# A delta-rule attention with a mixture of experts behind it: the first two triangular solves go from GpSimd to VectorE

## The chip, the cores and the metric
The kernel runs on one core of a Trainium2 chip. Five engines work side by side, each on its own instruction list in order: PE (TensorE, matmul), ACT (ScalarE), DVE (VectorE), POOL (GpSimd) and SP (SyncE, which here issues nearly all DMAs). They meet through semaphores. The metric is the device time in microseconds; before the change the median of three runs is 1027.19 us.

## The reference
Attention with a recurrent 40x40 state for each of 4 batches x 8 heads over 768 steps, then a top-2 mixture of 8 experts:

```python
for t in range(S):
    y[:, :, t] = einsum('bhd,bhde->bhe', r_t, state)
    Sa = einsum('bhde,bhe->bhd', state, a_t)
    state = state * w_t[:, :, None, :] - einsum('bhd,bhe->bhde', Sa, b_t) + einsum('bhd,bhe->bhde', v_t, k_t)
# x = y as [3072, 320]; logits = x @ w_gate, noise_scale = log1p(exp(x @ w_noise)),
# noisy = logits + noise_scale * noise; top 2 of 8 by noisy, softmax of the two;
# out = sum over the two experts of weight * (relu(x @ w1[e]) @ w2[e])
```

## The kernel before
The recurrence is done in chunks of 64 steps. The 12 chunks of 2 batch pairs (p = 0, 1) make 24 iterations (`for n in range(N)` in `run`), which run in order, since each hands the state on to the iteration two later of its pair. Four iterations (two chunks of both pairs) form a group g = 0 to 5, which is prepared together:

- `prepA(p,g)` loads w, b and a (`raww`, `rawba`), forms running products of w (`Gx`, a scan on VectorE), their inverses and the scaled operands, writes them to DRAM as pairs of 16-bit numbers (`pk` to `d_ab`) and reads them back stacked (`st_ab`). `rawba` and `Gx` have one buffer each, so that the next pair's load waits for the last use by this one. In groups 0 and 1 the two products of `rawba` run on VectorE, later on POOL.
- `scoresL` forms the 32x32 blocks on PE and writes them to DRAM (`scr<-lt`, `scr<-lo`) for both pairs.
- `tsolve(g)` reads them as one tile `X` (128 partitions, one 32x32 triangular matrix each, one buffer), masks it (L535), sets the diagonal (L536) and inverts it in 30 pairs of dependent instructions (L541 the outer product into `Tt`, L542 its sum into `X`). A pair j works on j x (31-j) elements, 30 to 240. The result goes to `th` (ACT L544, then VectorE L545), to DRAM, and from there into `dT`, four DMAs for each iteration (`fetchB`, L567).
- `prepC(p,g)` does the same as prepA for k (`rawk`).

An iteration (`chain`, then `outp`, and `pre` and `blocks` for the next) needs its `dT`: in `chain` the first application (PE pQ), a second block column, the split `w2` (ACT L598, VectorE L599, the second of the two `w` of an iteration), the second application, and the new state (L652). Iteration 0 needs group 0's solve, iteration 4 group 1's, iteration 8 group 2's.

The order on each engine is set once, when the program is built, by a scheduler that works from priorities and a model of times: what stands first in an engine's list runs first, and an instruction that waits holds up all behind it. `high_priority(offset)` puts instructions ahead in that choice; `add_manual_dep` without a semaphore only fixes an order. After the 24 iterations the experts run (some 450 us, nearly all PE); the change doesn't touch them.

Of the kernel before, what the change touches and what calls it, by code (L numbers as in the profile page):

```python
# [13 lines left out]
ALU = mybir.AluOpType  # L14
# [330 lines left out]
NP,NG,CG,C=2,6,2,64  # L345
# [3 lines left out]
SC=2.0**9; IS=2.0**-9  # L349
# [19 lines left out]
def host_tm(x):  # L369

    B,H,S,D=x.shape
    return np.ascontiguousarray(x[:,HS].reshape(NP,2,H,NG*CG,C,D).transpose(0,3,1,4,2,5)).reshape(NP,NG*CG,128,H*D)

class Att:
    PSC=1; PACC=3; PT=2; PPB=1
    def __init__(s,nc,tc,ctx,aps):
# [45 lines left out]
        for z in s.Sst+[s.Ut]: nc.vector.memset(z,0.0)  # L422
        s.dm=t([128,320],F16,name="dm"); nc.vector.memset(s.dm,0.0)

    def pack(s,src,scl,h,nc_,out):

        nc=s.nc
        pk=s.tmp.tile([120,nc_*2,X//nc_],F16,name="pk",bufs=PKB)
        v=pk.rearrange("p (c l) x->p c l x",l=2); sv=src.rearrange("p (c x)->p c x",c=nc_)
        nc.scalar.activation(v[:,:,h],sv,AF.Copy,scale=scl)  # L430
        nc.vector.scalar_tensor_tensor(v[:,:,1-h],sv,scl,v[:,:,h],op0=ALU.mult,op1=ALU.subtract)
        out(pk)
    def burst(s,f):

# [20 lines left out]
            return st[:,o:o+128] if b is None else st[:,o+64*b:o+64*b+64]  # L455
        return f
    def prepA(s,p,g):
        nc=s.nc; FM=s.aps[0]
        sh=[120,NS,64]; W0=NS*65
        w=s.inp.tile([120,W0],F32,name="raww",bufs=2); nc.sync.dma_start(w,FM[p,g][:,:W0])  # L460
        ba=s.inp.tile([120,2*X],F32,name="rawba",bufs=BAB)
        for i in range(2): nc.sync.dma_start(ba[:,X*i:X*i+X],FM[p,g][:,W0+X*i:W0+X*i+X])
        b_,a_=ba[:,:X],ba[:,X:]
        Gx=s.tmp.tile([120,NS,65],F32,name="Gx")
        fl=lambda z: z.rearrange("p a b->p (a b)")
        nc.vector.tensor_tensor_scan(fl(Gx),w,fl(s.d1),0.0,op0=ALU.mult,op1=ALU.add)
# [22 lines left out]
        (nc.vector if g in MD else nc.gpsimd).tensor_tensor(b_,b_,fl(NH),op=ALU.mult)
        s.pack(b_,-SC,1,1,lambda pk: nc.sync.dma_start(dv[:,:,1],pk))  # L490
        (nc.vector if g in MD else nc.gpsimd).tensor_tensor(a_,a_,fl(NG_),op=ALU.mult)
        s.pack(a_,-SC,0,1,lambda pk: nc.sync.dma_start(dv[:,:,0],pk))
# [12 lines left out]
    def prepC(s,G,gate=None):
        nc=s.nc; FM=s.aps[2]; p,g=G['p'],G['g']
# [171 lines left out]
    def run(s,m,xo=None):  # L678
        nc=s.nc
# [25 lines left out]
        with after(xd),(after(tl) if TG else ExitStack()):  # L705
            prepA(1,0); prepA(1,1); prepT(1)
# [3 lines left out]
        for n in range(N):  # L710
            g,c,p,cc=idx(n); ga,qa=divmod(n+LA,4); gc,qc=divmod(n+LC,4)
# [27 lines left out]
PT_=0; PA_=0  # L739
# [13 lines left out]
MD=(0,1); MG=(); MK=(0,); TG=0  # L753
# [128 lines left out]
```

## Time and profile before

| what | us |
|---|---|
| median of 3 timed runs (1023.14 to 1027.94) | 1027.19 |
| profiled execution | 1021.33 |
| its span, first to last instruction | 1019.5 |
| first `w2` of iteration 0 on VectorE | 152.24 |
| the last iteration's output `xt` on VectorE | 571.23 |

Busy over the span: PE 767.5 us (75%), DVE 492.1 (48%), ACT 396.1 (39%), POOL 521.4 (51%). These shares average over three stages that differ: up to 153 us almost nothing but preparation, from 153 to 571 us the iterations with the later groups' preparation between them, then the experts.

### The profile page before, as it was taken

The page shows a single profiled execution, that of the slowest core. Times are in us where ns is not written, and L with a number is a line of the kernel's source. Part 1 is how long each engine was busy: PE and PEld are TensorE (multiplying, and loading weights), DVE is VectorE, ACT ScalarE, POOL GpSimd, SP SyncE. Part 2 cuts the span into 40 slices and gives each one's busy share as a digit, 9 for nine tenths or more (in the row PEclk, how much of TensorE's full clock was granted, in tenths as well). Part 3 has the DMA queues.
Part 4 walks back from the last instruction along what each step waited for, and adds up shares of the span by engine and source line. Part 5 has one row for each costly group of instructions (what it writes and reads, how often), then busy time and mean ns, then how long its engine had stood idle before and what let it go on. Part 6 is the DMA issues. An engine that isn't in the chain of part 4 may idle for free.

```text
span 1019.5 us, 25178 instructions
## 1 busy us (share of the span) xinstructions
PE 767.5 (75%) x10506; PEld 681.2 (67%) x10506; DVE 492.1 (48%) x961; ACT 396.1 (39%) x816; POOL 521.4 (51%) x678
## 2 busy tenths in 40 slices
PE   0110117687877687899799379999999999999995
PEld 0110116576666576787688259899999989999995
DVE  9329525355567556447355542643434334443430
ACT  2213213354444344554454322543434334343421
POOL 6259979237967728818874335133333333333313
PEclk9999999797778787999899779999999999999998
DMA  3799963478479557655355843426262525262303
GB/s 96 188 203 226 242 172 90 116 197 225 127 193 241 146 121 204 175 152 146 96 120 148 272 119 68 131 49 150 49 150 49 150 49 149 50 149 51 36 7 40
DMA packets 135264, 136.21 MB, mean 134 GB/s; under 512 B 67392, under 2 KB 114948, under 8 KB 135060
## 3 DMA queue, kind: packets, MB, share of 16 engines
q1 hardware_dynamic: 123492, 117.35, 43.6%
q0 software_dynamic: 11648, 17.15, 9.6%
q8 instruction: 85, 1.39, 0.6%
q14 instruction: 39, 0.32, 0.1%
HBM read 96.48 MB, written 41.37 MB: 135 GB/s over the span
## 4 chain that ended last, share of the span: by engine, by line
PE 43%; POOL 21%; DMA 14%; issue 8%; DVE 6%; SPq 3%; ACT 3%; POOLq 0%; DVEq 0%; ACTq 0%
PE po L295 16%; PE ph L273 12%; POOL Tt L541 7%; POOL X L542 7%; PE pY L441 2%; PE psc L441 2%; PE pW L441 2%; DMA X<-scr 2%; DMA xr<-xd,le 2%; DMA out_dram<-y,le 2%; DMA d_ab<-pk 2%; DMA rawk<-in_fm_dram 2%; PE pt L254 2%; POOL rawk L515 2%; POOL xr L241 1%
## 5 line engine op out<-in xcount | busy, mean ns | idle before, releaser
L297 POOL DMA_INDIRECT out_dram<-y,le x56 | 92.4, 1651 | 201.2 <-ACT y L296 171.9
L276 DVE SCALAR_TENSOR_TENSOR hl<-ph,hh 128x256 fp32r<-128x256 f32 (+1 forms) x128 | 71.0, 556 | 154.0 <-ACT hh L274 153.6
L274 ACT ACTIVATE hh<-ph 128x320 fp32r<-128x320 f32 (+1 forms) x128 | 66.1, 518 | 156.1 <-PE ph L273 155.9
L541 POOL TENSOR_TENSOR Tt<-X 128x30 f32<-128x30 f32 (+9 forms) x180 | 108.8, 604 | 11.8
L542 POOL TENSOR_TENSOR X<-X,Tt 128x30 f32<-128x30 f32 (+9 forms) x180 | 106.3, 590 | 12.6
L241 POOL DMA_INDIRECT xr<-xd,le x56 | 54.0, 965 | 74.4 <-DMA le<-ls 27.9
L441 PEld LDWEIGHTS <-st_ab 120*64 120x64 f16 (+1 forms) x928 | 26.5, 117 | 75.8 <-issue 42.2
L295 PE MATMUL po<-w2h,hh 128*128 128x320 f32 x384 | 74.6, 314 | 0.0
L441 PE MATMUL pQ<-w,dT 128*128 128x40 f16 x1152 | 41.2, 184 | 42.3 <-DMA dT<-scr 33.5
L273 PE MATMUL ph<-xh,w1h 128*128 128x512 f32 (+1 forms) x256 | 71.3, 362 | 0.5 <-ACT xh L257 0.5
L441 PEld LDWEIGHTS <-dT 128*128 128x128 f16 x1152 | 38.2, 100 | 49.6 <-DMA dT<-scr 34.4
L273 PE MATMUL ph<-xh,w1l 128*128 128x512 f32 (+1 forms) x256 | 69.0, 351 | 0.0
L273 PE MATMUL ph<-xl,w1h 128*128 128x512 f32 (+1 forms) x256 | 68.6, 349 | 0.0
L295 PE MATMUL po<-w2l,hh 128*128 128x320 f32 x384 | 68.3, 312 | 0.0
L295 PE MATMUL po<-w2h,hl 128*128 128x320 f32 x384 | 68.1, 309 | 0.0
L441 PE MATMUL psc<-st_ab 120*64 120x64 f16 x384 | 12.6, 215 | 68.1 <-DMA st_ab<-d_ab 29.6
L295 PEld LDWEIGHTS po<-w2h,hh 128*128 128x128 f32 x384 | 61.3, 188 | 3.1
L441 PE MATMUL psc<-RV,uT 128*64 128x128 f32 x384 | 56.5, 294 | 4.1 <-DVE P L665 3.7
L295 PEld LDWEIGHTS po<-w2h,hl 128*128 128x128 f32 x384 | 59.2, 188 | 0.1
L295 PEld LDWEIGHTS po<-w2l,hh 128*128 128x128 f32 x384 | 58.9, 188 | 0.4
L162 POOL DMA_INDIRECT ls<-ent,po x48 | 47.2, 984 | 19.3 <-issue 13.6
L441 PE MATMUL psc<-RV 128*64 128x128 f32 x384 | 56.6, 294 | 0.0
(285 smaller groups left out, 1893.9 us busy)
## 6 DMA issues: line engine op xcount, KB each, us to landing
w2r<-in_w_dram SPq DMA_DIRECT2D x8, 1280.0 KB
RV<-in_rv_dram SPq DMA_DIRECT2D x48, 192.0 KB
rawba<-in_fm_dram SPq DMA_DIRECT2D x24, 360.0 KB
d_ab<-pk SPq DMA_DIRECT2D x24, 360.0 KB
st_ab<-d_ab SPq DMA_DIRECT2D x36, 240.0 KB
w1r<-in_w_dram SPq DMA_DIRECT2D x8, 1024.0 KB
raww<-in_fm_dram SPq DMA_DIRECT2D x12, 365.6 KB
st_ab<-d_ab SPq DMA_DIRECT2D x24, 180.0 KB
```

The source lines that it names most:

```text
L162: st=nc.gpsimd.indirect_dma_start(out=s.ls[s.half],out_offset=OFFS(ap=po[:,j,k:k+1],axis=0),in_=s.ent[:,j,k],in_offset=None)
L241: for k in range(c,c+a): nc.gpsimd.indirect_dma_start(out=x[:p,k],out_offset=None,in_=s.xd[w],in_offset=OFFS(ap=li[:p,k,0:1],axis=0))
L254: for t,p in tiles(t0,n): nc.tensor.transpose(pt[:,t-t0:t-t0+p],x[:p,t//128,f0:f0+128],s.idm[:p,:p])
L273: for i,(a,b) in enumerate(mm): nc.tensor.matmul(ph[:,:n],a,b,start=i==0,stop=i==7)
L274: nc.scalar.activation(hh[:,f,:n],ph[:,:n],AF.Relu)
L276: if c.stop>c.start: nc.vector.scalar_tensor_tensor(o,ph[:,c],0.0,hh[:,f,c].bitcast(F32),op0=ALU.max,op1=ALU.subtract)
L295: nc.tensor.matmul(po[:p],h[:,f,r],w[:,f],start=k==0,stop=k==23); k+=1
L297: st=nc.gpsimd.indirect_dma_start(out=s.out_d,out_offset=OFFS(ap=idx[:p,ii],axis=0),in_=y[:p],in_offset=None,compute_op=ALU.add)
L441: def mm(s,*a,**k): return lambda: s.nc.tensor.matmul(*a,**k)
L515: k1=k_[:,:,:,64*b:64*b+64]; (nc.vector if g in MK else nc.gpsimd).tensor_tensor(k1,k1,G['NH'].rearrange("p (a c b) t->p b c a t",a=3,c=CG ...
L541: eng.tensor_tensor(t,Xt[:,j:j+1,j+1:].to_broadcast([128,j,m]),Xt[:,0:j,j:j+1].to_broadcast([128,j,m]),op=ALU.mult)
L542: s.tl=eng.tensor_tensor(Xt[:,0:j,j+1:],Xt[:,0:j,j+1:],t,op=ALU.add)
```

## The change
All solves ran on POOL (`TPOOL`); now those of groups 0 and 1 run on VectorE. Group 0's gets a high priority offset, and a wrapper puts every VectorE instruction of group 1's `prepA` behind the last step of group 0's solve in VectorE's list. The rest of `prepA`'s lines change `nc.vector` to the wrapped `V`. In the changed kernel lines from L374 on stand 11 lower (L541 is L552), and the wrapped instructions are recorded at L380.

```diff
+class Behind:
+    def __init__(s,tc,eng,first): s.tc,s.eng,s.first=tc,eng,first
+    def __getattr__(s,name):
+        f=getattr(s.eng,name)
+        def g(*a,**k):
+            i=f(*a,**k)
+            s.tc.add_manual_dep(i.ins,s.first.ins.name,mybir.DependencyInfo(mybir.DependencyClass.NoSync,mybir.DependencyReason.DATA),reason="behind")
+            return i
+        return g
...
     def prepA(s,p,g):
-        nc=s.nc; FM=s.aps[0]
+        nc=s.nc; FM=s.aps[0]; V=Behind(s.tc,nc.vector,s.tl) if g==1 else nc.vector
...
-        nc.vector.tensor_tensor_scan(fl(Gx),w,fl(s.d1),0.0,op0=ALU.mult,op1=ALU.add)
+        V.tensor_tensor_scan(fl(Gx),w,fl(s.d1),0.0,op0=ALU.mult,op1=ALU.add)
...
         def prepT(g):
-          with s.tc.high_priority(offset=PT_):
+          with s.tc.high_priority(offset=PT_ if g else BURST):
             scr2[g]=s.tsolve(scr[g],nc.gpsimd if g in TPOOL else nc.vector)
...
-TPOOL=(0,1,2,3,4,5)
+TPOOL=(2,3,4,5)
```

VectorE's list at the place of group 0's solve, before: the last two scalings of k for group 0, then `ak` and `w` of iteration 0, `wg` (a constant of the experts' gate, loaded by DMA), `ak` of iteration 1, and group 1's `prepA` from `Gx` on.

```order
L431 SCALAR_TENSOR_TENSOR pk<-rawk,pk 120x2x384
L515 TENSOR_TENSOR rawk<-rawk,NH 120x6x64 x2
L431 SCALAR_TENSOR_TENSOR pk<-rawk,pk 120x2x384
L580 TENSOR_TENSOR ak<-psc,mk_124 128x512
L599 SCALAR_TENSOR_TENSOR w_870<-pW,w_870 128x320
L60 SCALAR_TENSOR_TENSOR wg<-wgn,wg 128x48
L580 TENSOR_TENSOR ak<-psc,mk_124 128x512
L466 SCALAR_TENSOR_TENSOR Gx<-raww,d_108 120x780
L472 TENSOR_TENSOR NH<-Gx,raww 120x768
L474 SCALAR_TENSOR_TENSOR raww<-NH,raww 120x768
L475 TENSOR_TENSOR NH<-raww,Gx 120x768
L482 TENSOR_TENSOR nge_556<-Gx,raww 120x12
```

The same place now (`X` and `Tt` are the solve's; `w`, `wg` and `ak` the same as above):

```order
L552 TENSOR_TENSOR Tt<-X 128x150
L553 TENSOR_TENSOR X<-X,Tt 128x6x25
L552 TENSOR_TENSOR Tt<-X 128x168
L553 TENSOR_TENSOR X<-X,Tt 128x7x24
L552 TENSOR_TENSOR Tt<-X 128x184
L610 SCALAR_TENSOR_TENSOR w_870<-pW,w_870 128x320
L60 SCALAR_TENSOR_TENSOR wg<-wgn,wg 128x48
L553 TENSOR_TENSOR X<-X,Tt 128x8x23
L591 TENSOR_TENSOR ak<-psc,mk_124 128x512
L552 TENSOR_TENSOR Tt<-X 128x198
L553 TENSOR_TENSOR X<-X,Tt 128x9x22
L552 TENSOR_TENSOR Tt<-X 128x210
```

The 62 instructions of the solve stand between the scalings of k and group 1's `Gx`; the two `ak`, `w` and `wg` stand inside it, and `Gx` comes after its last step.

VectorE's list at group 1's solve, before: iterations 1 and 2 (`w_1648` is iteration 2's first split, `Sst_171` the state after iteration 1, `P` the masked scores of iteration 1's output) and group 3's `prepA`, and in it `th` of group 1, which waits for POOL's solve.

```order
L599 SCALAR_TENSOR_TENSOR w_1648<-pW,w_1648 128x320
L474 SCALAR_TENSOR_TENSOR raww<-NH,raww 120x768
L652 SCALAR_TENSOR_TENSOR Sst_171<-pS,gam_146 128x8x40
L475 TENSOR_TENSOR NH<-raww,Gx 120x768
L482 TENSOR_TENSOR nge_2520<-Gx,raww 120x12
L445 COPY uT<-pu 128x512
L606 TENSOR_TENSOR sfs<-Sst_171,sfs 128x320
L481 COPY nge_4046<-nge_2520 120x6
L545 SCALAR_TENSOR_TENSOR th<-X,th 128x1024
L665 TENSOR_TENSOR P<-psc,mk 128x512
L431 SCALAR_TENSOR_TENSOR pk<-rawba,pk 120x768
L665 TENSOR_TENSOR P<-psc,mk 128x512
```

Now, at the start of that solve:

```order
L109 SCALAR_TENSOR_TENSOR xT<-px,xT 128x384
L442 SCALAR_TENSOR_TENSOR pk<-rawba,pk 120x768 x2
L663 SCALAR_TENSOR_TENSOR Sst_171<-pS,gam_146 128x8x40
L546 TENSOR_TENSOR X<-X,tri 128x1024
L617 TENSOR_TENSOR sfs<-Sst_171,sfs 128x320
L610 SCALAR_TENSOR_TENSOR w_1648<-pW,w_1648 128x320
L547 MEMSET X 128x32
L552 TENSOR_TENSOR Tt<-X 128x30
L456 COPY uT<-pu 128x512
L553 TENSOR_TENSOR X<-X,Tt 128x30
L552 TENSOR_TENSOR Tt<-X 128x58
L514 COPY gam_145<-pg 128x9x2
```

The 62 instructions of the solve now stand in VectorE's list from behind `Sst_171` of iteration 1 on; between its mask and its last step stand 28 others, 16 of iterations 1 to 3 and 12 of preparation. In front of its mask, all of group 1's and most of group 2's `prepA` stand between the two solves, mixed with iterations 0 and 1: 14 instructions of these from iteration 0's `w2` on.

SyncE's list at the load of group 1's matrix, before (`scr_433<-th` is group 0's inverse, `dT` its use in iterations 0 to 2):

```order
L492 DMA d_ab<-pk 120x2x768
L462 DMA rawba<-in_fm_dram 120x768 x2
L518 DMA d_k<-pk 120x4x384
L509 DMA rawk<-in_fm_dram 120x768
L534 DMA X<-scr 128x1024
L547 DMA scr_433<-th 128x2048
L567 DMA dT_147<-scr_433 32x8x64 x4
L567 DMA dT_148<-scr_433 32x8x64 x4
L567 DMA dT_147<-scr_433 32x8x64 x4
```

Now (`xd<-xt` is iteration 0's output, `dT_148` in front the load for iteration 3):

```order
L540 DMA scr<-lt 32x16x32
L540 DMA scr<-lo 32x16x32
L529 DMA d_k<-pk 120x4x384
L105 DMA xd_840<-xt 128x320
L578 DMA dT_148<-scr_433 32x8x64 x3
L545 DMA X<-scr 128x1024
L578 DMA dT_148<-scr_433 32x8x64
L506 DMA st_ab<-d_ab 80x1536 x3
L507 DMA st_ab<-d_ab 40x3x768
L501 DMA d_ab<-pk 120x2x768
```

Group 1's matrix stood ahead of group 0's inverse; now it stands behind iteration 0's output and three of the four loads of iteration 3, which wait until iteration 1 has used the same buffer.

## Rows read from the trace of the kernel before

**Rows 1.** Stages: from:to, us, busy us (instructions) by engine, granted clock, DMA share, GB/s
```profile
56.00:153.00 97.00, 12.49 (x246) 10.58 (x247) 51.05 (x50) 23.27 (x37) 79.01 (x95) 1.00 0.85 210
153.00:240.00 87.00, 63.13 (x1429) 53.37 (x1427) 45.13 (x71) 36.99 (x84) 50.14 (x69) 0.85 0.58 146
```

**Rows 2.** The page's chain that ended last: shares of the span by engine, by line
```profile
PE 43%; POOL 21%; DMA 14%; issue 8%; DVE 6%; SPq 3%; ACT 3%; POOLq 0%; DVEq 0%; ACTq 0%
PE po L295 16%; PE ph L273 12%; POOL Tt L541 7%; POOL X L542 7%; PE pY L441 2%; PE psc L441 2%; PE pW L441 2%; DMA X<-scr 2%; DMA xr<-xd,le 2%; DMA out_dram<-y,le 2%; DMA d_ab<-pk 2%; DMA rawk<-in_fm_dram 2%; PE pt L254 2%; POOL rawk L515 2%; POOL xr L241 1%
```

**Rows 3.** POOL in order of time: start, us, instruction, count, [idle before, releaser]
```profile
56.39 2.12 POOL L535 TENSOR_TENSOR X<-X,tri 128x1024 f32<-128x1024 f32 x1 [23.87 <-DMA X<-scr]
136.26 0.27 POOL L542 TENSOR_TENSOR X<-X,Tt 128x30 f32<-128x30 f32 x1
141.13 1.94 POOL L515 TENSOR_TENSOR rawk<-rawk,NH 120x384 f32<-120x384 f32 x2 [4.61 <-DMA rawk<-in_fm_dram]
144.27 2.12 POOL L535 TENSOR_TENSOR X<-X,tri 128x1024 f32<-128x1024 f32 x1 [1.19 <-DMA X<-scr]
163.02 0.70 POOL L542 TENSOR_TENSOR X<-X,Tt 128x240 f32<-128x240 f32 x1
184.75 1.81 POOL L489 TENSOR_TENSOR rawba<-rawba,NH 120x768 f32<-120x768 f32 x1
209.18 1.49 POOL L477 TENSOR_TENSOR NG__2518<-Gx,raww 120x768 f32<-120x768 f32 x1 [22.62 <-PE pgm L442]
210.75 3.36 POOL L491 TENSOR_TENSOR rawba<-rawba,NG__2518 120x768 f32<-120x768 f32 x1
```

**Rows 4.** VectorE in order of time, 60 to 153 us
```profile
60.01 0.69 DVE L580 TENSOR_TENSOR ak<-psc,mk 128x512 f32<-128x512 f32 x1 [9.41 <-PE psc L441]
63.23 0.49 DVE L599 SCALAR_TENSOR_TENSOR w<-pW,w 128x320 f16<-128x320 f32 x1 [2.53 <-ACT w L598]
68.21 0.55 DVE L60 SCALAR_TENSOR_TENSOR wg<-wgn,wg 128x48 f16<-128x48 f32 x1 [4.48 <-ACT wg L59]
69.51 2.19 DVE L466 TENSOR_TENSOR_SCAN Gx<-raww,d 120x780 f32<-120x780 f32 x1 [0.16 <-DMA raww<-in_fm_dram]
73.53 0.96 DVE L472 TENSOR_TENSOR NH<-Gx,raww 120x768 f32<-120x768 f32 x1 [1.83 <-ACT raww L470]
74.53 0.96 DVE L474 SCALAR_TENSOR_TENSOR raww<-NH,raww 120x768 f32<-120x768 f32 x1
90.41 1.77 DVE L489 TENSOR_TENSOR rawba<-rawba,NH 120x768 f32<-120x768 f32 x1 [0.46 <-DMA rawba<-in_fm_dram]
137.92 1.30 DVE L545 SCALAR_TENSOR_TENSOR th<-X,th 128x1024 f16<-128x1024 f32 x1 [1.85 <-ACT th L544]
152.24 0.49 DVE L599 SCALAR_TENSOR_TENSOR w<-pW,w 128x320 f16<-128x320 f32 x1 [13.03 <-ACT w L598]
```

**Rows 5.** SyncE's DMA issues in order of time, groups 0 and 1
```profile
116.16 0.48 SPq L529 DMA_DIRECT2D scr<-lo  x1
139.25 0.36 SPq L534 DMA_DIRECT2D X<-scr  x1
145.42 10.75 SPq L567 DMA_DIRECT2D dT<-scr  x12
```

**Rows 6.** VectorE and POOL side by side, 465 to 467 us
```profile
465.14 0.21 DVE L177 TENSOR_TENSOR zc<-zc,lg 128x64 f32<-128x64 f32 x1
466.29 0.47 POOL L542 TENSOR_TENSOR X<-X,Tt 128x150 f32<-128x150 f32 x1
466.34 0.50 DVE L178 TENSOR_TENSOR L__6619<-L__6619,d 128x64 f32<-128x64 f32 x1
```

**Rows 7.** VectorE in order of time, group 1's inverse and iteration 4
```profile
186.23 1.49 DVE L545 SCALAR_TENSOR_TENSOR th<-X,th 128x1024 f16<-128x1024 f32 x1 [8.57 <-ACT th L544]
223.36 0.49 DVE L599 SCALAR_TENSOR_TENSOR w<-pW,w 128x320 f16<-128x320 f32 x1 [0.88 <-ACT w L598]
```

**Rows 8.** SyncE's DMA issue of group 2's matrix
```profile
217.55 0.34 SPq L534 DMA_DIRECT2D X<-scr  x1
```

More of the change, by code (lines that the diff above doesn't have):

```diff
@@ L423, in consts, with pack @@
         s.dm=t([128,320],F16,name="dm"); nc.vector.memset(s.dm,0.0)
-    def pack(s,src,scl,h,nc_,out):
+    def pack(s,src,scl,h,nc_,out,V=None):
         nc=s.nc
@@ L430, in pack @@
         nc.scalar.activation(v[:,:,h],sv,AF.Copy,scale=scl)
-        nc.vector.scalar_tensor_tensor(v[:,:,1-h],sv,scl,v[:,:,h],op0=ALU.mult,op1=ALU.subtract)
+        (V or nc.vector).scalar_tensor_tensor(v[:,:,1-h],sv,scl,v[:,:,h],op0=ALU.mult,op1=ALU.subtract)
         out(pk)
@@ L471, in prepA @@
         NH=s.tmp.tile(sh,F32,name="NH",bufs=2)
-        nc.vector.tensor_tensor(NH,P,r0,op=ALU.mult)
+        V.tensor_tensor(NH,P,r0,op=ALU.mult)
         nr=r0
-        nc.vector.scalar_tensor_tensor(nr,NH,2.0,r0,op0=ALU.subtract,op1=ALU.mult)
-        nc.vector.tensor_tensor(NH,nr,P[:,:,31:32].to_broadcast(sh),op=ALU.mult)
+        V.scalar_tensor_tensor(nr,NH,2.0,r0,op0=ALU.subtract,op1=ALU.mult)
+        V.tensor_tensor(NH,nr,P[:,:,31:32].to_broadcast(sh),op=ALU.mult)
         NG_=s.tmp.tile(sh,F32,name="NG_",bufs=NGB)
-        s.pl=(nc.vector if g in MG else nc.gpsimd).tensor_tensor(NG_,Gx[:,:,0:64],nr[:,:,31:32].to_broadcast(sh),op=ALU.mult)
+        s.pl=(V if g in MG else nc.gpsimd).tensor_tensor(NG_,Gx[:,:,0:64],nr[:,:,31:32].to_broadcast(sh),op=ALU.mult)
         nge=s.tmp.tile([120,CG+1,3,2],F32,name=f"nge{p}",bufs=2)
         v4=lambda z: z.rearrange("p (a c b) t->p c a b t",a=3,c=CG)
-        if g==0: nc.vector.memset(nge[:,0],0.0)
-        else: nc.vector.tensor_copy(nge[:,0],s.nge[p][:,CG])
-        nc.vector.tensor_tensor(nge[:,1:CG+1],v4(Gx)[:,:,:,:,64],v4(nr)[:,:,:,:,31],op=ALU.mult)
+        if g==0: V.memset(nge[:,0],0.0)
+        else: V.tensor_copy(nge[:,0],s.nge[p][:,CG])
+        V.tensor_tensor(nge[:,1:CG+1],v4(Gx)[:,:,:,:,64],v4(nr)[:,:,:,:,31],op=ALU.mult)
         s.nge[p]=nge
         gm=s.tmp.tile([120,2,3,CG],F32,name="gm")
-        nc.vector.tensor_tensor(gm.rearrange("p b a c->p c a b"),nge[:,0:CG],v4(Gx)[:,:,:,:,32],op=ALU.mult)
+        V.tensor_tensor(gm.rearrange("p b a c->p c a b"),nge[:,0:CG],v4(Gx)[:,:,:,:,32],op=ALU.mult)
         G={'p':p,'g':g,'NH':NH,'ng':NG_.rearrange("p (a c b) t->p a c (b t)",a=3,c=CG),'gm':gm}
@@ L488, in prepA @@
         dv=d.rearrange("l p x n->p l x n")
[L489 to L492, printed above, removed]
+        (V if g in MD else nc.gpsimd).tensor_tensor(b_,b_,fl(NH),op=ALU.mult)
+        s.pack(b_,-SC,1,1,V=V,out=lambda pk: nc.sync.dma_start(dv[:,:,1],pk))
+        (V if g in MD else nc.gpsimd).tensor_tensor(a_,a_,fl(NG_),op=ALU.mult)
+        s.pack(a_,-SC,0,1,V=V,out=lambda pk: nc.sync.dma_start(dv[:,:,0],pk))
         st=s.sab[(2*g+p)%SAB].tile([120,18*K],F16,name="st_ab")
@@ L502, in prepA @@
         gv=s.gam[p][:,:,g*CG:(g+1)*CG]
-        nc.vector.tensor_copy(gv,pg.rearrange("p q (a c)->p (q a) c",a=3))
+        V.tensor_copy(gv,pg.rearrange("p q (a c)->p (q a) c",a=3))
         return G
```

## The prediction

> **What bounds the kernel now.** I read the stages first. Between 56 and 153 us PE is busy 12.5 us of 97, POOL 79 and VectorE 51, with the DMA engines at 0.85: PE has next to nothing to do. From 153 us PE is busy 63 us of 87 [rows 1]. So the iterations start at about 150 us, and everything before is a lead-in. The chain that ended last tells who sets it: outside the experts' lines (L295, L273) its largest shares are the two lines of the solve on POOL, 7% each [rows 2]. That is an average over six solves, so I then went to each engine in order of time. POOL starts group 0's mask at 56.39 us and ends its last step at 136.53. Group 1's solve starts at 144.27 and is over when the next instruction starts at 184.75: 40.5 us nearly unbroken, against 80.1 for the first, which shares POOL with preparation and collides with VectorE [rows 3]. VectorE's half of `th` ends at 139.22, the first application's result passes VectorE as `w2` at 152.24, which is 13.0 us for the write to DRAM, `dT` and one application [rows 4]. Taking the first solve off POOL therefore attacks a real wait of 80 us. The question is what is late next.
>
> **Step 1: group 0's solve on VectorE.** No row shows a solve step there, so I size it by rows of two-input instructions: 768 elements take 0.96 us [rows 4], 64 take 0.21 when POOL isn't in the way [rows 6]. That is 0.142 us and 1.065 ns an element. Dependent neighbours start 1.00 us apart at 0.96 long, a gap of 0.04 [rows 4]. The 60 steps have 2 x 4,960 = 9,920 elements: 8.5 + 10.6 + 2.4 = 21.5 us, or 0.36 a step, and with mask (1.2) and diagonal (0.1) 22.9 us. Bounds: nothing excludes that the fixed part of a step is hidden, which leaves 10.6 + 1.3 = 12 us; at the upper end a step costs what POOL needs, 40.5 us. I take 22.9, which the nearest rows give.
>
> The Trainium skill, GPSIMD Engine Reference, section "Elementwise — side-by-side cycle accounting", puts GpSimd at 1.96 times VectorE's time for a two-input instruction. By that estimate a solve takes 40.5 / 1.96 = 20.7 us instead of 22.9, and the sum below would be some 4 us better; no row here has the step on both engines.
>
> The solve isn't wholly unbroken. Inside it stand two `ak` (0.69), `w` (0.49) and `wg` (0.55), 2.4 us. The first `ak` waits for PE until 60.0 (0.8 us later than the solve reaches it), and `wg` waits until 68.2 for its DMA by way of ACT [rows 4]; the solve reaches it at about 64.5, so 3.7 us go there. End: 56.4 + 22.9 + 2.4 + 4.5 = 86.2 us, 50 us earlier. `Gx` (about 1.8 without collision) covers ACT's half of `th`, then two small copies and VectorE's half: 89.6. With the same 13.0 us, iteration 0's `w2` comes at 102.6 instead of 152.24. That is the 50 us which the change seems to promise.
>
> **Step 2: group 1's preparation pays.** Before, `Gx` of group 1 starts at 69.51 [rows 4] and its last score block is issued at 116.16 [rows 5], say 118 landed: 49 us. Its matrix X is loaded only at 139.25, since the one X buffer is in use until `th` is done [rows 5]. So before the change group 1's data lie ready for 20 us. Now `Gx` starts at 86.2, and between the two solves 14 instructions of iterations 0 and 1 stand in VectorE's list. At 0.64 us (45.13 us over 71 instructions, [rows 1]) they cost 9 us. Against that, VectorE's large instructions ran at up to 1.77 instead of 0.96 beside POOL's solve [rows 4], and POOL is now quiet: I give back 5 us. X's data are there at 86.2 + 49 + 9 - 5 = 139. SyncE has three `dT` of iteration 3 ahead of the load, so it is issued at about 140, and the mask starts at 145, as the 5.0 us from 139.25 to 144.27 say [rows 3, 5]. Before it started at 144.27. The 50 us are gone for group 1: its solve starts no earlier than before.
>
> **Step 3: group 1's solve shares VectorE with iterations 1 to 3.** 22.9 us of solve and 28 others at 0.64 make 40.7; POOL has 1.9 + 1.8 + 1.5 + 3.4 = 8.6 us of group 3's and 2's preparation there [rows 3], of which I count half as collision, 4.3 (bounds 0 and 8.6). What collides shows at 466 us: 64 elements take 0.50 on VectorE, ending with POOL's instruction, instead of 0.21 [rows 6]. The last step is then at 190; one `P`, ACT's half of `th` (1.4) and VectorE's (1.3) follow: 193.4, against 187.7 before [rows 7]. So group 1's inverse is 6 us later than before. But iterations 0 to 3 no longer wait for it or hold it: before, iteration 4's `w2` came only at 223.36 [rows 7], 36 us after the inverse, because iterations 0 to 3 had started at 150 and had still to be done. Now they lie in VectorE's list ahead of it. With 13.0 us from `th` to `w2`, iteration 4 has it at 206.4, 17 us earlier.
>
> The Trainium skill, SBUF — State Buffer, section "Who interferes with whom", says that a VectorE instruction with two SBUF inputs contends with a GpSimd instruction that reads SBUF, and that the later one is fully blocked. Both solve lines are of this kind, so the rule speaks against moving them while POOL prepares: by it all of the 8.6 us may count, and iteration 4 gains 13 us. The trace agrees in the one place shown, 0.50 us for 0.21.
>
> **Step 4: what carries on.** Group 2's solve stays on POOL. Its X stands behind two `dT` of iteration 4, first issued 6.2 us after `th` (139.22 to 145.42, [rows 4, 5]) and 0.9 apart: 201.4, against 217.55 [rows 8]. So both what iteration 4 waits for and what iteration 8 waits for move by 16 to 17 us, and VectorE's later list is nearly the same. I take 16 us through to the end; the experts' 450 us stay. That POOL has two solves fewer I count at nothing beyond this, as it sits idle for 22.6 us ahead of group 3's work at 209 anyway [rows 3].
>
> **The sum.** 1021.3 (the profiled execution, a span of 1019.5 and 1.8 around it) - 16 = 1005.3. The three runs lie 1.8 to 6.6 above that execution, the median 5.9. On the median's scale the forecast is 1011; I name 1008, between the two.
>
> **Rivals.** A: the 50 us stay in larger part. For it: of the 49 us of group 1's preparation much is collision and waiting for POOL, and PE, idle then, can't be the cause. Against it: the chain from load to `d_ab`, `st_ab` and scores is a row of DMA turns, which no faster engine shortens. If it takes 33 us instead of 49, X is there at 129, iteration 4 is 33 us earlier: 988, on the scale named 991. Chance 0.2.
> B: no net change. The DMA engines are at 0.85 in the lead-in [rows 1], and the same transfers now meet the loads of iterations 0 to 3. Four turns for each pair (`rawba`, `d_ab`, `st_ab`, `scr`), 2 us longer each, are 16 us for the two pairs of group 1: X at 161, and iteration 4's `w2` at 222, as before: 1021 to 1027. Chance 0.15.
> C: slower. One mechanism: the step on VectorE. All 120 steps stand before group 1's inverse, the first 60 by step 2 as well. A gain of 16.5 us is used up at 0.14 us more a step, 0.50 in place of 0.36. For it: each step waits on its forerunner's semaphore, and the collision costs 0.3 an instruction [rows 6]. Against it: the gap of 0.04, and that POOL is quiet in the first solve. At POOL's own 0.64 a step (40.5 less the mask's 2.1, over 60) 34 us are added: 1039, on the scale named 1042. Chance 0.15.
> That the change doesn't do what it says is settled by the order, as far as it goes: four instructions stand inside the first solve, priced above.
>
> **Chances.** Forecast 0.5, its own range 998 to 1018; A 0.2, B 0.15, C 0.15. The range 985 to 1034 takes in the forecast, most of A, B and the near part of C. A difference under 0.5%, 5 us, can't be told from none: faster 0.70 (the forecast and A), same 0.15 (B and the forecast's edge, less the part of B that falls outside), slower 0.15.
>
> **What would show it.** Step 1: the first solve's steps near 0.36 us, a stop of some 4 us at `wg`, iteration 0's `w2` near 103. Step 2: group 1's X loaded near 140, no earlier than before; if near 128, A. Step 3: the second solve 40 to 50 us from mask to `th`, iteration 4's `w2` near 206. Step 4: group 2's X near 201. The forecast is wrong if the steps average over 0.5 us, or if iteration 4's gain is lost again by iteration 8.

## The result

The changed kernel takes 1015.8 us in the median of 4 runs, the kernel before 1025.2 in the median of 4 on the same chip: a ratio of 0.9896, interval 0.9862 to 0.993, so about 10.7 us faster. The forecast was 1008, with faster as the likeliest side; 16 us of gain were expected, two thirds of that came.

The execution that was profiled is not one to take the total from: it took 1026.0 us at a mean granted clock of 0.892, its three fellows 1010.8 to 1016.7 at 0.91 to 0.92. Up to 210 us its stages can still be read against [rows 1 to 8], since a second trace of the changed kernel has the same points there within about 1 us (group 2's X at 197.5 instead of 198.5). For what comes later both kernels were profiled again on another chip, which runs both 47 to 50 us slower.

VectorE in order of time, changed kernel, first chip (start us, us, then engine, line, operation; in brackets the idle time before it and what ended that). `L546` is the mask, `L552` and `L553` the two lines of a solve step, `w` at 101.11 and 209.07 the split `w2` of iterations 0 and 4:

```profile
56.50 1.23 DVE L546 TENSOR_TENSOR X<-X,tri 128x1024 f32<-128x1024 f32 x1 [6.21 <-DMA X<-scr]
...
67.07 0.21 DVE L60 SCALAR_TENSOR_TENSOR wg<-wgn,wg 128x48 f16<-128x48 f32 x1 [3.07 <-ACT wg L59]
...
84.75 0.21 DVE L553 TENSOR_TENSOR X<-X,Tt 128x30 f32<-128x30 f32 x1
...
86.69 1.29 DVE L556 SCALAR_TENSOR_TENSOR th<-X,th 128x1024 f16<-128x1024 f32 x1
...
101.11 0.49 DVE L610 SCALAR_TENSOR_TENSOR w<-pW,w 128x320 f16<-128x320 f32 x1
...
147.87 1.22 DVE L546 TENSOR_TENSOR X<-X,tri 128x1024 f32<-128x1024 f32 x1 [1.17 <-DMA X<-scr]
...
172.47 0.41 DVE L552 TENSOR_TENSOR Tt<-X 128x240 f32<-128x240 f32 x1
...
175.25 1.08 DVE L553 TENSOR_TENSOR X<-X,Tt 128x238 f32<-128x238 f32 x1
...
190.13 1.30 DVE L556 SCALAR_TENSOR_TENSOR th<-X,th 128x1024 f16<-128x1024 f32 x1
...
209.07 0.49 DVE L610 SCALAR_TENSOR_TENSOR w<-pW,w 128x320 f16<-128x320 f32 x1 [1.22 <-ACT w L609]
```

The first solve runs from 56.50 to 84.96 us and `th` is done at 87.98, where POOL needed until 136.53 [rows 3]. Iteration 0 has its `w2` at 101.11 instead of 152.24 [rows 4]. Group 1's solve starts at 147.87, no earlier than the 144.27 of POOL [rows 3]; its inverse is done at 191.43. Iteration 4 has its `w2` at 209.07 instead of 223.36 [rows 7]: of 51 us at iteration 0, 14 are left at iteration 4.

SyncE's issues, same kernel and chip:

```profile
138.93 0.51 SPq L540 DMA_DIRECT2D scr<-lo  x1
...
142.65 1.41 SPq L578 DMA_DIRECT2D dT<-scr  x3
144.16 0.38 SPq L545 DMA_DIRECT2D X<-scr  x1
...
198.46 0.34 SPq L545 DMA_DIRECT2D X<-scr  x1
```

Group 1's X follows 5.2 us behind its last score block (138.93 to 144.16), with iteration 0's output and three `dT` between them; before, that block was out at 116.16 and X waited for the buffer until 139.25 [rows 5]. Group 2's X is loaded at 198.46 instead of 217.55 [rows 8].

Busy time by stage (PE, PEld, VectorE, ACT, POOL in us, then granted clock, DMA share, GB/s), same kernel and chip:

```profile
56.00:153.00 97.00, 38.35 (x663) 33.31 (x664) 77.87 (x139) 30.83 (x60) 20.12 (x12) 0.90 0.82 202
153.00:240.00 87.00, 70.53 (x1334) 59.70 (x1330) 61.38 (x121) 36.22 (x79) 40.85 (x46) 0.70 0.78 192
```

Against [rows 1] the lead-in has changed hands: VectorE 78 of 97 us instead of 51, POOL 20 instead of 79, and PE is busy 38 us instead of 12, with work that stood behind the first solve.

**Where the lead goes.** Traces of both kernels on the second chip. Earlier by, in us: group 2's X 20.2 (217.7 to 197.5), iteration 8's output 23.6 (336.6 to 313.0), group 3's X 12.9 (290.7 to 277.8), group 3's `th` 10.4 (356.2 to 345.8), iteration 9's output 13.8 (362.1 to 348.3), group 4's X 12.6, group 5's `th` 12.6, iteration 22's output 12.0, the end 9.1 (spans 1072.3 and 1063.2). So a lead of some 20 us (11.5 to 28.7 by iteration) is there up to iteration 8, and 10 us of it go between iterations 8 and 9. VectorE there, before:

```profile
354.94 1.30 DVE L545 SCALAR_TENSOR_TENSOR th<-X,th 128x1024 f16<-128x1024 f32 x1 [4.78 <-ACT th L544]
...
361.63 0.49 DVE L676 TENSOR_TENSOR xt<-pY,xt 128x320 f32<-128x320 f32 x1
```

and changed:

```profile
344.32 1.48 DVE L556 SCALAR_TENSOR_TENSOR th<-X,th 128x1024 f16<-128x1024 f32 x1 [9.82 <-ACT th L555]
...
347.80 0.48 DVE L687 TENSOR_TENSOR xt<-pY,xt 128x320 f32<-128x320 f32 x1
```

`xt` is iteration 9's output, which needs nothing of group 3. It stands behind group 3's `th` in VectorE's list, and `th` waits for POOL's solve. ACT stands there longer still, on its half of `th`, and through ACT so does PE: group 4's score blocks (`psc<-st_ab`) are copied out by ACT (`lo`, L527 before, L538 changed), this copy stands behind `th` in ACT's list, and the next matmuls wait for it, with a product that iteration 9's output needs (`pgm`) behind them in PE's list. ACT and PE before:

```profile
353.57 1.33 ACT L544 ACTIVATE th<-X 128x1024 f16<-128x1024 f32 x1 [5.87 <-POOL X L542]
356.79 0.64 PE L441 MATMUL psc<-st_ab 120*64 120x64 f16 x16 [5.18 <-ACT lo L527]
```

and changed:

```profile
342.92 1.37 ACT L555 ACTIVATE th<-X 128x1024 f16<-128x1024 f32 x1 [12.37 <-POOL X L553]
344.83 0.64 PE L452 MATMUL psc<-st_ab 120*64 120x64 f16 x16 [16.77 <-ACT lo L538]
```

So PE stands idle there for 16.8 us instead of 5.2, and by this trace that is the wait which ends last: `xt` starts 2 us behind the end of `th`, once PE and ACT have passed on its other operand. The iterations came 20 us earlier, group 3's solve on POOL only 10.

### The profile page after: what moved, and what is told of

It reads as the page before. It is cut to its first block, busy times and chain, and to the rows that moved or that the text cites. A ratio compares the mean times of both kernels' runs of the same rounds, so it can differ in the third digit from the quotient of the medians.

```text
span 1024.3 us, 25163 instructions
## 1 busy us (share of the span) xinstructions
PE 799.3 (78%) x10506; PEld 708.9 (69%) x10506; DVE 528.0 (52%) x1085; ACT 397.9 (39%) x816; POOL 439.7 (43%) x554
## 4 chain that ended last, share of the span: by engine, by line
PE 49%; DMA 17%; POOL 12%; DVE 10%; issue 6%; SPq 3%; ACT 2%; POOLq 0%; ACTq 0%; DVEq 0%
PE po L295 16%; PE ph L273 14%; POOL X L553 4%; POOL Tt L552 4%; DMA rawk<-in_fm_dram 3%; PE psc L452 3%; PE pY L452 3%; PE pW L452 2%; DMA d_ab<-pk 2%; DMA xr<-xd,le 2%; DMA le<-ls 2%; POOL xr L241 2%; PE pt L254 2%; PE pQ L452 1%; DVE X L553 1%
## 5 line engine op out<-in xcount | busy, mean ns | idle before, releaser
L553 POOL TENSOR_TENSOR X<-X,Tt 128x30 f32<-128x30 f32 (+14 forms) x120 | 69.1, 576 | 8.1
L552 POOL TENSOR_TENSOR Tt<-X 128x30 f32<-128x30 f32 (+14 forms) x120 | 67.7, 564 | 7.8
L452 PE MATMUL psc<-RV,uT 128*64 128x128 f32 x384 | 65.4, 325 | 7.0 <-DVE P L676 6.6
L452 PE MATMUL psc<-RV 128*64 128x128 f32 x384 | 65.4, 325 | 0.0
L452 PEld LDWEIGHTS psc<-RV,uT 128*64 128x64 f32 x384 | 51.6, 164 | 16.1 <-DVE P L676 7.7
L676 DVE TENSOR_TENSOR P<-psc,mk 128x512 f32<-128x512 f32 x48 | 33.0, 687 | 54.7 <-PE psc L452 54.7
L162 POOL DMA_INDIRECT ls<-ent,po x48 | 47.4, 987 | 19.5 <-issue 14.1
L296 ACT ACTIVATE y<-po,le 128x320 f32<-128x320 f32 x48 | 25.4, 529 | 73.3 <-PE po L295 73.3
```

The costliest lines, as they stand in the source:

```text
L162: st=nc.gpsimd.indirect_dma_start(out=s.ls[s.half],out_offset=OFFS(ap=po[:,j,k:k+1],axis=0),in_=s.ent[:,j,k],in_offset=None)
L296: nc.scalar.activation(y[:p],po[:p],AF.Copy,scale=w_[:p,ii:ii+1])
L452: def mm(s,*a,**k): return lambda: s.nc.tensor.matmul(*a,**k)
L552: eng.tensor_tensor(t,Xt[:,j:j+1,j+1:].to_broadcast([128,j,m]),Xt[:,0:j,j:j+1].to_broadcast([128,j,m]),op=ALU.mult)
L553: s.tl=eng.tensor_tensor(Xt[:,0:j,j+1:],Xt[:,0:j,j+1:],t,op=ALU.add)
L676: nc.vector.tensor_tensor(m,pp.rearrange("p i j t->p (i j) t"),s.mk.to_broadcast([128,8,64]),op=ALU.mult)
```

## The experiments

None ran on the first chip. The first eight ran on the second, `th_pool`, `end_order` and `solve3_end` on a third, `x_first` on a fourth. The kernel before takes 1072.6 to 1074.8 us in the median on each of these three, so times within traces are compared between them too; ratios are always to the kernel before on the same chip, with 95% interval. Line numbers of a kernel shift by the lines that its edit adds.

**The changed kernel and the kernel before once more** (no edit).

> The changed kernel once more, for a closer ratio and a second trace. Theory 1 (the lead of iterations 4 to 8 is lost again on the way, by VectorE's list waiting for POOL's later solves and by what stands at the handover to the experts): 0.987 to 0.993 of before, i.e. 7 to 13 us; the outputs of iterations 0 to 8 come some 16 us earlier than before, those from iteration 13 on within 5 us of before. Rival (the loss seen in the first trace came from its lower granted clock alone): where the clock is at before's level, the lead of 16 us is there up to iteration 23 and the run is at 0.984 or better.

Measured: 0.9915, 0.9881 to 0.9948, as expected. The course is only half as expected: the outputs of iterations 13 to 22 still come 12.0 to 13.3 us earlier, not within 5 us of before, so half the lead stays in this trace, where the first chip's, of the execution set aside above, has none left at iteration 13 (433.5 against 433.9). The rival on the clock is not settled by it, since the granted clock is again lower than before's (0.892 against 0.915); `x_first` below bears on it.

> The kernel before once more, for a trace from the chip on which the others of this call run. All theories expect the order of the first trace: group 2's X loaded right behind its own last score block and iteration 2's output, group 3's behind iteration 6's, group 4's behind iteration 10's; group 1's inverse some 25 us or more ahead of group 2's X.

Measured: one run, 1074.0 us, span 1072.3. X of group 2 at 217.7 follows the score block of 214.9 and iteration 2's output at 211.3, group 3's at 290.7 iteration 6's at 289.9, group 4's at 382.7 iteration 10's at 380.3; group 1's inverse is done at 188.2. As expected.

**Only the first solve.**

```diff
-TPOOL=(2,3,4,5)
+TPOOL=(1,2,3,4,5)
```

> Only group 0's solve runs on VectorE, unbroken, group 1's stays on POOL. Theory 1 (what pays is that iterations 0 to 3 are done before group 1's inverse; its X is bounded by its preparation at about 144 us): X of group 1 loaded at 140 to 146 us; the solve on POOL takes 41 to 50 us, th at 190 to 200; gain 6 to 13 us, as with both solves moved (0.987 to 0.994). Rival (the second solve on VectorE is what pays): th of group 1 past 205 us and 0.995 to 1.000.

Measured: 1.0001, 0.9979 to 1.0022, the rival's range. My theory of that time falls: nothing is gained. Its X of group 1 came at 143.9, as expected, but SyncE shows what holds group 2's X:

```profile
188.32 0.50 SPq L540 DMA_DIRECT2D scr<-lo  x1
...
211.49 0.36 SPq L558 DMA_DIRECT2D scr<-th  x1
211.95 1.02 SPq L545 DMA_DIRECT2D X<-scr  x1
```

The scores of group 2 are out at 188.8, earlier than in any other kernel, and X waits 23 us for the one buffer, that is for `th` of group 1, since POOL's solve, with eight other products in its list, takes from 147.8 to 207.2.

**Only the second solve.**

```diff
-        nc=s.nc; FM=s.aps[0]; V=Behind(s.tc,nc.vector,s.tl) if g==1 else nc.vector
+        nc=s.nc; FM=s.aps[0]; V=nc.vector
-          with s.tc.high_priority(offset=PT_ if g else BURST):
+          with s.tc.high_priority(offset=PT_):
-TPOOL=(2,3,4,5)
+TPOOL=(0,2,3,4,5)
```

> Only group 1's solve runs on VectorE, group 0's stays on POOL as before. Theory 1: the iterations start at 150 us as before and VectorE now has 23 us more to do between iterations 0 to 3: no gain or slower, 1.000 to 1.012. Rival (POOL's relief is what pays, its later preparation and solves come earlier): 0.990 to 0.996.

Measured: 1.0015, 0.999 to 1.004, within the theory's range: POOL's relief alone gains nothing either. Here group 1's `th` is done at 175.6, and X of group 2 waits for the other thing: its last score block, issued at 208.6, because the scores stand beside iteration 2 (output at 205.5). SyncE:

```profile
175.62 0.34 SPq L558 DMA_DIRECT2D scr<-th  x1
...
208.61 0.49 SPq L540 DMA_DIRECT2D scr<-lo  x1
...
211.90 0.34 SPq L545 DMA_DIRECT2D X<-scr  x1
```

**Both solves, without the unbroken order** (the first two edits of the one above, `TPOOL` as changed).

> Both solves on VectorE, but group 0's without the rank ahead of group 1's preparation: VectorE's instructions of that preparation stand between its steps. Theory 1 (the end of group 1's inverse sets the time, not that of group 0's): group 0's inverse later by the 15 to 25 us of the instructions in between, X of group 1 at 125 to 138, the time the same or better than with the order (0.980 to 0.992). Rival (the unbroken order is what pays): 0.995 to 1.005 of before, slower than the changed kernel by 5 us or more.

Measured: 0.9896, 0.9865 to 0.9927, as good as the changed kernel. The first inverse is done at 125.8 instead of 88.9, group 1's X is loaded at 125.8 instead of 144.2, group 2's at 206.9 instead of 197.5. That group 1's preparation pays for the unbroken solve is shown by this pair; the order as such is worth nothing that can be measured. It also shows that the full lead at group 2's X isn't needed for the gain: here this X comes only 10.8 us earlier than before (217.7 to 206.9), there 20.2, and the end comes to the same.

So group 2's X comes when both are there, the scores (which follow iteration 2) and the free buffer (which follows group 1's `th`): 214.9 and 188.2 before, 188.8 and 211.5 with the first solve alone, 209.1 and 175.6 with the second alone, 194.2 and 191.8 with both. Either move alone leaves the other wait in place: X then comes at 211.9 in both, 5.8 us earlier than before, and nothing of that reaches the end.

**Group 3's solve on VectorE as well.**

```diff
-TPOOL=(2,3,4,5)
+TPOOL=(2,4,5)
```

> The changed kernel with group 3's solve on VectorE as well. Theory 2 (from group 2 on a loop sets the pace: X is loaded behind the scores that stand in the lists beside iteration 4g-6, POOL solves, VectorE's half of th stands in its list ahead of iteration 4g-3, and so on to the next X): the solve of group 3, 68 us on POOL between X and th, takes 30 to 45 us, so th of group 3 comes at 308 to 325 us instead of 346 to 350, group 4's X 15 to 30 us earlier, and the time is 0.968 to 0.982 of before. Rival (VectorE itself is the bound there, or the lead of the changed kernel is lost for another reason, such as the clock): 0.988 to 1.000.

Measured: 0.9816, 0.9775 to 0.9856. VectorE in order of time:

```profile
331.73 1.27 DVE L556 SCALAR_TENSOR_TENSOR th<-X,th 128x1024 f16<-128x1024 f32 x1
...
338.26 0.48 DVE L687 TENSOR_TENSOR xt<-pY,xt 128x320 f32<-128x320 f32 x1
```

`th` waits no more, iteration 9's output comes 9.6 us earlier than in the changed kernel, group 4's X at 360.1, 10 earlier (15 to 30 were expected). The solve took 56.5 us from X to `th`, not 30 to 45: VectorE is busy 50 of the 57 us. The direction and the ratio were right, the price of the steps among the iterations' work too low.

**The preparation's products on VectorE.**

```diff
-MD=(0,1); MG=(); MK=(0,)
+MD=(0,1,2,3,4,5); MG=(); MK=(0,1,2,3,4,5)
```

> The changed kernel with the products of the preparation (rawba, rawk) of groups 2 to 5 on VectorE too, so that POOL has only the solves, NG_ and the small transfers. Theory 2: the solves 2 to 5 take 41 to 48 us from X to th instead of 46 to 68, th of group 2 at 240 to 248 us, and the time is 0.965 to 0.983 of before. Rival (VectorE now stands waiting for the loads that these products wait for, with the iterations behind it in the list): the solves are shorter, the outputs of the iterations come no earlier, 0.990 to 1.005.

Measured: 0.9991, 0.9958 to 1.0023, as the rival had it. POOL's solves are shorter as expected (49.6 us for group 2 instead of 67.5, 57.8 for group 3 instead of 68.0), but group 1's `th` comes at 216.5 instead of 191.8, with ten of these products in VectorE's list in between and 6.1 us of waits for `rawk` among them. The gain is spent before it begins.

**All six solves on VectorE.**

```diff
-TPOOL=(2,3,4,5)
+TPOOL=()
```

> The changed kernel with all six solves on VectorE. Theory 2: the loop is shorter by 15 to 30 us in each of groups 2 and 3 and by 10 to 20 in 4, none in 5: 0.945 to 0.972 of before, until iteration time on TensorE (16 us) sets the pace. Rival (with 92 us more of solves VectorE is the bound from 153 us on): 0.990 to 1.010.

Measured: 0.9797, 0.9755 to 0.984, short of what was expected, and not to be told from `solve3`. Between X and `th` group 2 takes 67.4 us and group 3 79.9, no less than on POOL: VectorE is busy 56 of 68 us in the one and waits 14.3 us at one `P` in the other. That wait isn't VectorE's own: POOL, free of solves, issues the first 16 of the routing's 32 small transfers (`DMA_INDIRECT`) there, and PE, on which `P` waits, issues its matmuls slowly meanwhile, as the last section describes:

```profile
340.50 0.96 POOL L162 DMA_INDIRECT ls<-ent,po  x1 [0.30 <-issue]
343.21 0.19 PE L452 MATMUL ptr<-cmb,st_k 120*128 120x40 f16 x1 [1.84 <-issue]
344.22 0.69 DVE L676 TENSOR_TENSOR P<-psc,mk 128x512 f32<-128x512 f32 x1 [14.27 <-PE ptr L452]
```

So group 3's 79.9 us don't price a solve on VectorE. Iteration 17's output is 34.6 us later than in the changed kernel (514.7), iteration 18's 11.4 earlier (527.6): what it gains comes in that stage, where only the other 16 transfers are left (from iteration 16's output to 18's 44.6 us instead of 70.7). No run moves the transfers alone.

**`th` off the lists of ACT, VectorE and SyncE.**

```diff
-        nc.scalar.activation(th[...,0],Xt,AF.Copy,scale=SC)
-        nc.vector.scalar_tensor_tensor(th[...,1],Xt,SC,th[...,0],op0=ALU.mult,op1=ALU.subtract)
+        if eng is nc.gpsimd:
+            eng.tensor_scalar(Xt,Xt,SC,None,op0=ALU.mult); eng.tensor_copy(th[...,0],Xt)
+            eng.tensor_tensor(th[...,1],Xt,th[...,0],op=ALU.subtract)
+        else: ...
-        s.nc.sync.dma_start(scr2...
+        (nc.gpsimd if eng is nc.gpsimd else nc.sync).dma_start(scr2...
```

> The changed kernel, but for groups 2 to 5, whose solves are on POOL, both halves of th and th's store to DRAM are on POOL too (three instructions on 1,024 elements in place of ACT's one and VectorE's one). Theory 2 (the iterations of a group lose their lead because th, which waits for POOL's solve, stands ahead of iteration 9's and 13's instructions in the lists of ACT, VectorE and SyncE): iteration 9's output at 328 to 340 us instead of 348, iteration 10's at 345 to 356 instead of 368, group 4's X at 350 to 358 instead of 370, the time 0.970 to 0.985 of before, although each inverse comes 3 to 5 us later. Rival (iteration 9 waits for something else that comes at the same time): outputs as in the changed kernel or later, 0.988 to 1.000.

Measured: 0.9884, 0.9835 to 0.9934, which is the rival's range. In the middle it still does what was expected: iteration 9's output at 336.7, iteration 10's at 355.4, group 4's X at 358.4. At the end it gives this back, and POOL shows where:

```profile
539.83 0.32 POOL L133 TENSOR_TENSOR acc<-acc,lg 128x64 f32<-128x64 f32 x1 [22.57 <-ACT lg L115]
540.11 2.34 POOL L556 TENSOR_TENSOR th<-X,th 128x1024 f16<-128x1024 f32 x1
...
557.80 0.60 POOL L561 DMA_DIRECT2D scr<-th  x1
```

In POOL's list the last group's `th` now stands among the routing's 32 small transfers and behind a sum that waits 22.6 us for the logits; its store goes out at 557.8, where the changed kernel has it at 490.1. Iteration 20's output is 14.6 us later than there.

**The first expert's split behind the last output.** In the changed kernel `w1l`, which waits for its load, stands ahead of the last iteration's output in VectorE's list, in the kernel before behind it.

```diff
+        Att.xl=nc.vector.tensor_tensor(xout, ...)      # the iteration's output
-            x=s.loadx(0); W1=s.split1(r1); X=s.trans(x[0])
+            x=s.loadx(0); W1=s.split1(r1,Behind(s.tc,nc.vector,Att.xl)); X=s.trans(x[0])
```

> The changed kernel with VectorE's part of the first expert's w1 split put behind the last iteration's output in VectorE's list, as it stood in the kernel before. Theory (w1l, waiting for its load, holds up the last iteration): the last output comes 12 to 13 us after the one before it instead of 18.6, 610 to 616 us on this chip, and 2 to 9 us of that reach the end: 0.982 to 0.989. Rival (the experts wait for the same load anyway): the output comes earlier, the experts start no earlier, and the time is that of the changed kernel, 0.989 to 0.994.

Measured: 0.9933, 0.9904 to 0.9963, as the rival had it. The first expert's matmuls (all of them in one line: count, durations, first and last start), changed kernel and this one:

```profile
L273 PE MATMUL ph<-xh,w1h x256: 305/389/793, 635.4 to 1033.2; 128*128 128x512 f32 x64, 128*128 128x320 f32 x64
```

```profile
L273 PE MATMUL ph<-xh,w1h x256: 305/389/796, 644.8 to 1041.6; 128*128 128x512 f32 x64, 128*128 128x320 f32 x64
```

The last two outputs lie 10.3 us apart instead of 18.6, but the experts start 23.6 us behind the last output instead of 13.6. From iteration 22's output to the experts' start it is 32 us in the changed kernel, 34 here and 32 before: the order at the last output doesn't move that start. That the load sets it is the likeliest reading, not shown by itself.

**Both of these.** The edits of `solve3` and `end_order`.

> Both: group 3's solve on VectorE (0.9816 alone) and the split behind the last output. Theory 2 with the end effect: 0.973 to 0.980. If the experts wait for the load anyway: 0.979 to 0.985.

Measured: 0.9869, 0.9821 to 0.9918, above both expected ranges: no better than `solve3` alone (0.9775 to 0.9856), which agrees with the result above.

**Group 3's X ahead in SyncE's list.** In the changed kernel the load comes 12.8 us behind `th` of group 2, in the kernel before 5.0. SyncE in the kernel before, and in the changed one:

```profile
285.72 0.35 SPq L547 DMA_DIRECT2D scr<-th  x1
...
289.12 1.44 SPq L567 DMA_DIRECT2D dT<-scr  x3
290.74 0.34 SPq L534 DMA_DIRECT2D X<-scr  x1
```

```profile
265.03 0.35 SPq L558 DMA_DIRECT2D scr<-th  x1
...
267.75 1.42 SPq L540 DMA_DIRECT2D scr<-lo  x1
269.26 1.93 SPq L578 DMA_DIRECT2D dT<-scr  x4
...
271.73 1.95 SPq L578 DMA_DIRECT2D dT<-scr  x4
...
274.21 0.49 SPq L540 DMA_DIRECT2D scr<-lo  x1
...
277.80 0.34 SPq L545 DMA_DIRECT2D X<-scr  x1
```

Eight `dT` transfers have got between the score blocks.

```diff
             i_=s.nc.sync.dma_start(d[32*i:32*i+32, ...
+            if G["g"]==2 and c==0: s.tc.add_manual_dep(i_.ins,s.xd.ins.name, ... ,reason="behind")
```

> The changed kernel with one edit in SyncE's list: the eight dT transfers of iterations 8 and 9 stand behind the load of group 3's X instead of between its score blocks. In the changed kernel that load comes 12.8 us after th of group 2, before the change 5.0. Theory 2 (the loop X, solve, th, scores of the next group sets the pace, and the lead is lost first in SyncE's list): X of group 3 at 270 to 273 us instead of 277.8, th of group 3 5 to 7 us earlier (339 to 341), iteration 9's output 341 to 344, the time 0.982 to 0.988 of before. Rival (the solve then waits for POOL's products in between, whose loads come no earlier, or iteration 8 is late for its dT): X early but th of group 3 and iteration 9's output as in the changed kernel, 0.988 to 0.995.

Measured: 0.977, 0.9742 to 0.9799, better than expected, and not for the reason expected. SyncE, VectorE and POOL of this kernel:

```profile
273.09 0.35 SPq L545 DMA_DIRECT2D X<-scr  x1
273.49 4.99 SPq L578 DMA_DIRECT2D dT<-scr  x8
```

```profile
333.67 0.48 DVE L688 TENSOR_TENSOR xt<-pY,xt 128x320 f32<-128x320 f32 x1
...
342.92 1.31 DVE L556 SCALAR_TENSOR_TENSOR th<-X,th 128x1024 f16<-128x1024 f32 x1 [2.66 <-ACT th L555]
```

```profile
311.64 0.64 POOL L553 TENSOR_TENSOR X<-X,Tt 128x240 f32<-128x240 f32 x1
...
319.94 1.95 POOL L526 TENSOR_TENSOR rawk<-rawk,NH 120x384 f32<-120x384 f32 x2 [5.51 <-DMA rawk<-in_fm_dram]
```

X is loaded 4.7 us earlier, but `th` comes only 1.6 earlier (344.2), because the solve stands still behind a product that waits 5.5 us for `rawk`. So far the rival was right. But the scheduler laid out the later lists anew: iteration 9's output now stands ahead of `th` in VectorE's list, ACT copies group 4's score blocks out at 327 to 330 us, ahead of its half of `th` (341.5), PE has no wait of 5 us or more there, and the output comes at 334.2 instead of 348.3, group 4's X at 356.9 instead of 370.1, group 5's `th` at 475.8 instead of 490.1, and the span is 15.9 us shorter. By this trace the gain is that of the order at `th`, not of the earlier load; no run has the order without the load. This is the fastest kernel of the study, 1048.4 us against 1073.9 before, measured on the fourth chip alone, so the differences in us just given are between two chips.

## Why the prediction was right, and where it was not

**Step 1 held.** The solve ended at 84.96 (86.2 forecast), the stop at `wg` was 3.07 us (3.7), iteration 0's `w2` came at 101.11 (102.6). A 240-element instruction took 0.41 us (0.40 by the two-point fit). One of the two points was misread: the 0.21 us of [rows 6] had POOL's solve beside it as well (steps at 464.76 to 465.17 and from 465.25), so that row doesn't show what it was read for; the price it gave held all the same, 0.22 us at 58 elements. On POOL 240 elements take 0.64 (the line at 311.64 above), a ratio of 1.6. The Trainium skill, GPSIMD Engine Reference, section "Elementwise — side-by-side cycle accounting", gives 1.96; at this size the measurement stands below it.

**Step 2 held.** Group 1's X came at 144.16 (140), its mask at 147.87 (145): no earlier than before. Kernel `plain` shows the exchange from the other side.

**Step 3 held, and rests on more than it said.** `th` came at 191.43 (193.4), iteration 4's `w2` at 209.07 (206.4). That `th` is so near is in part luck: the solve began 2.9 us later than forecast and took 40.7 us from mask to last step, the sum without the 4.3 us of collision that were added to it. The collision is there where POOL works: beside

```profile
174.81 2.39 POOL L526 TENSOR_TENSOR rawk<-rawk,NH 120x384 f32<-120x384 f32 x2 [7.68 <-DMA rawk<-in_fm_dram]
```

(POOL of the changed kernel, first chip) two neighbouring solve instructions took 1.08 and 1.09 us instead of 0.41. The Trainium skill, SBUF — State Buffer, section "Who interferes with whom", has a VectorE instruction of this kind blocked by GpSimd's reads; this trace agrees. But the step told the gain as one of the iterations done ahead of `th`, as if the first solve alone gave it. `first_only` gains nothing, and I expected 6 to 13 us of it.

**Step 4 failed in one place.** "I take 16 us through to the end" is the term that was mis-sized: it measured 10.7 us on the first chip and 9.1 between the two profiled spans on the second. Group 2's X came even 19 us earlier (198.46 against 217.55), and iteration 8 kept all of that (23.6 us on the second chip). The sentence next to it, that two solves fewer on POOL count at nothing beyond this, held: POOL's solve of group 2 took 67.5 us from X to `th` instead of 68.0, that of group 3 68.0 instead of 65.5 (second chip). What `first_only` adds is how much hangs on the second solve: with it back on POOL, its end at 207.2 sets group 2's X, and the whole gain is gone. What I left out is the next solve on POOL. Group 3's `th` moved by 10.4 us only, and iteration 9 stands behind it in VectorE's list and, by way of ACT, in PE's. "VectorE's later list is nearly the same" passed over what stands in the lists behind a wait that moves less. What holds that solve is a product in POOL's list whose load is awaited, before and changed, second chip:

```profile
332.07 1.95 POOL L515 TENSOR_TENSOR rawk<-rawk,NH 120x384 f32<-120x384 f32 x2 [5.51 <-DMA rawk<-in_fm_dram]
```

```profile
320.51 0.99 POOL L526 TENSOR_TENSOR rawk<-rawk,NH 120x384 f32<-120x384 f32 x1 [6.43 <-DMA rawk<-in_fm_dram]
```

From the end of that wait to the end of `th` it is 24.1 us before, 25.3 in the changed kernel and 24.3 in `x_first` (319.94 to 344.2): the 11.6 us by which this load's product moved are what `th` moved by, within 1.2. That the lead is lost at `th` is shown by three kernels that take the wait for it away in different ways (`solve3`, `th_pool`, `x_first`): PE has no wait of 5 us or more there in any of them, and iteration 9's output comes 9.6, 11.6 and 14.1 us earlier than in the changed kernel. Two of them keep it to the end (0.9816 and 0.977); `th_pool` loses it at a place that its own trace names. My own check in the prediction, whether the gain is lost by iteration 8, was one iteration too early.

**The rivals.** A (more of the 50 us stays) and C (steps over 0.5 us) did not come. B named no net change through longer transfers: X came at 144 and not at 161, and the DMA engines were busy as long for a byte as before (0.82 at 202 GB/s, [rows 1] 0.85 at 210). The clock as the whole cause of the loss is refuted: `x_first` has a granted clock of 0.890, no higher than the changed kernel's 0.892, and is 15.9 us faster. Between iterations 8 and 9, where PE stands idle, the changed kernel's clock is 0.65 (before 0.73); what share of the rest it has is not separated.

**Open.** That `all_dve` has its gain from the routing's transfers, half of which it issues earlier, is read from its trace and was not tested, nor was what the awaited load of `rawk` is worth by itself. Where 12.0 us of lead at iteration 22 become 9.1 at the end is not taken apart. Whether the ratios of the experiments hold on the first chip is not known.

## What to carry to other kernels

When two waits meet at one buffer, moving either alone may gain nothing, as it did here: write down for each step all that it waits for, with its time, before pricing a move. A lead is worth what the next instruction in a list allows that waits for something which did not move; look in every list for work that stands behind such a wait without needing it, also in the list of an engine that waits only for the one that waits (here PE behind ACT), and take the wait out of its way. And an edit of a few transfers can lay out all later lists anew, so read the gain from the trace, not from the edit.

## What the runs showed of the hardware

The three other chips ran the kernel before 47 to 50 us slower than the first. Most of it is one stage. While POOL issues the routing's 32 small indirect transfers, one each 1.26 us, PE there issues its matmuls ever more slowly, in the end one each 1.4 to 2.1 us, with nothing that the profile shows to wait for:

```profile
512.51 0.19 PE L452 MATMUL ptr<-cmb,st_ab 120*128 120x40 f16 x1 [1.22 <-issue]
...
516.00 0.19 PE L452 MATMUL ptr<-cmb,st_ab 120*128 120x40 f16 x1 [1.88 <-issue]
```

(PE of the changed kernel, second chip.) From iteration 17's output to iteration 18's it takes 59 us there (480.1 to 539.0), in the kernel before 58 (492.8 to 551.0), and on the first chip 12 to 20. The same transfers run on the first chip with PE at work beside them. The slow stretch goes with the transfers: in `all_dve`, which issues 16 of them at 321 to 341 us, PE has such gaps there too. The cause is open; both kernels carry it, so the ratios stand (0.9896 on the one chip, 0.9915 on the other).
